# The first layer's first product as seven products on quadrants, in two PSUM banks per group

## The chip, the cores and the metric

The kernel runs on one core of one Trainium2 chip. The metric is the device time of one execution in microseconds (us). Of the core's engines, PE multiplies matrices, ACT and DVE work on vectors in the on-chip memory SBUF and in the accumulators of PSUM, POOL does a few reductions over partitions here, and SP issues the transfers. Each engine runs its own list of instructions in order; semaphores hold an instruction until others are done.

## The reference

Attention within chunks of 64 positions, then two feed-forward layers over 4608 tokens of width 512, each with 2048 hidden features:

```python
scores = scale * np.matmul(q_c, k_c.transpose(0, 1, 2, 4, 3))   # chunks of 64, 8 heads of 64
attn = np.exp(scores - np.max(scores, axis=-1, keepdims=True))
attn = attn / (np.sum(attn, axis=-1, keepdims=True) + 1e-09)
x = np.matmul(attn, v_c)                                        # as 4608 x 512
# first layer
h = x @ w_in
r = np.maximum(h, 0.0)
x = (s * (r * r) + b) @ w_out
# second layer
h = x @ w2_in
P = a[0] + a[1] * h + a[2] * h**2 + a[3] * h**3
Q = 1.0 + np.abs(b2[0]) * np.abs(h) + np.abs(b2[1]) * h**2
out = (P / (Q + 1e-06)) @ w2_out
```

## The kernel before

The tokens go in blocks: two of 256, computed in fp32 while the weights are still being made ready, then eight of 512 (j from 2 to 9). A hidden layer has 16 chunks f of 128 features. From block 2 on a product in near-fp32 precision is three fp16 matmuls (`TERMS`): an operand is split into a high half (a scaled copy, on ACT) and a low half (the rest, on DVE), and high x high, high x low and low x high are added in PSUM.

For a chunk f, `h_mm` (called by `l1_h`) runs 4 x 3 matmuls of 512 columns into one of two PSUM banks of the pool `ps_h`. ACT takes Relu of the bank into `r` (L429), squares it (L430) and writes its high half into `g` (L439); DVE subtracts for the low half (L440). The second product `l1_y` runs 12 matmuls of 512 columns that add chunk f into four PSUM banks `y`. In the program order the second product of a chunk comes one or two chunks after its first, so the other bank's product stands between.

The order is set by a list of slots, one for each chunk of each block (`seq1`). `at(slot, fn, ...)` files a job under a slot and `run_jobs` issues it there. So the softmax of the tiles of a later block, its scale c (`x_norm`, whose maximum over partitions is on POOL), its split into four pairs of halves (`x_split`, L379 and L380), the output of a finished block (`l1_out`, L474), its own scale and pieces for the second layer (`y_norm`, `y_split`) and the weights of the second layer are put between the chunks. These last are loaded raw from DRAM (`w2_load`, one load for two units of 128 x 512), decoded on DVE from 64-bit words to fp32 (L136 to L139: `bits`, `wf`) and written back ("parked"), during blocks 3 to 7. An amount `P0`, `PV0`, `WS`, `WP` sets how many slots before a block, or after which slot, such a job stands. ACT's chain for a tile of attention is L222, L236, L266 (exponential), L279 and L305 (x out of PSUM); DVE's is L264, L265, L273 to L280 and L306.

The second layer already has its first product by seven products on quadrants (Strassen's scheme in Winograd's form): a weight matrix and the input are both cut in 2 x 2 quadrants, seven sums or differences of the quadrants of each (`WORD` for the weights, `YORD` for the input) are split into halves, and seven products of half the size in each direction are added in three PSUM banks (`bZ`, `bY`, `bC`), with ACT copies between the banks. `PROD` names the two operands of each product. A unit of four chunks is a group there; its product form is L849.

What the two blocks of 256 tokens need first is the decoding of the first layer's weights in the order `units`, each through one of three buffers `bufs`; after them come the splits of these weights (`split`).

## Time and profile before

| | us |
|---|---|
| median of three runs | 1591.37 |
| lowest and highest run | 1589.68, 1595.19 |
| the profiled execution | 1593.01 |
| its span, first to last instruction | 1591.2 |
| PE busy | 1565.9 (98%) |
| DVE busy | 1232.2 (77%) |
| ACT busy | 921.8 (58%) |
| POOL busy | 25.7 (2%) |

The profile is of one execution; its rows give each instruction's or group's time, the idle time of its engine ahead of it, and what ended that idle time. The time from the first to the last instruction is 1.8 us under the time that was taken for this execution. The blocks of 512 tokens of the first layer run on PE from 149.5 to 870.6, the second layer from there to the end. A matmul's row overlaps the one behind it, so a run of twelve is measured from its start to the next one's start.

### The profile page before, as it was taken

To read this page: it belongs to the slowest core of one execution; us is meant where nothing else is said; L and a number is where in the kernel's file an instruction comes from. 1 tells how busy PE (TensorE), PEld (TensorE's weight loads), DVE (VectorE), ACT (ScalarE), POOL (GpSimd) and SP (SyncE) were. 2 spreads that over 40 slices of the span, in tenths; PEclk is the share of its full clock that TensorE was granted. 3 is DMA by queue.
4 is the path that set the end of the run, shared out by engine and by line. 5 is a ranking of instruction groups with operands and counts; after the bars stand their busy time and mean duration, and the time that the engine had idled before them with its cause. 6 is when DMAs were issued, how large, how long until landed. Compare 5 with 4: busy or idle time off the path is not lost.

```text
span 1591.2 us, 27221 instructions
## 1 busy us (share of the span) xinstructions
PE 1565.9 (98%) x11349; PEld 923.6 (58%) x11349; DVE 1232.2 (77%) x1886; ACT 921.8 (58%) x1296; POOL 25.7 (2%) x57
## 2 busy tenths in 40 slices
PE   8999999999999999999999899999999999999998
PEld 6887454444444444444445666666666666666664
DVE  7987448686777777364583999999998889888887
ACT  3676557374555646464675755555656565656564
POOL 0000000000000000000000000000000000000000
PEclk8999999999999999999999999999999999999999
DMA  7832216536354453111132010101010101010000
GB/s 283 280 87 76 52 42 199 172 108 178 107 165 136 136 149 98 42 34 54 54 114 86 34 60 27 47 27 47 27 47 27 48 27 47 27 47 34 20 27 27
DMA packets 86108, 131.27 MB, mean 83 GB/s; under 512 B 39648, under 2 KB 39648, under 8 KB 85984
## 3 DMA queue, kind: packets, MB, share of 16 engines
q1 hardware_dynamic: 85984, 129.53, 26.8%
q8 instruction: 89, 1.46, 0.4%
q14 instruction: 35, 0.29, 0.1%
HBM read 86.77 MB, written 34.34 MB: 76 GB/s over the span
## 4 chain that ended last, share of the span: by engine, by line
PE 73%; DVE 16%; issue 4%; DMA 4%; ACT 3%; POOL 0%; SPq 0%; POOLq 0%; ACTq 0%; DVEq 0%
PE y L907 19%; PE hp L414 16%; PE y L456 16%; PE bZ L849 9%; PE bY L849 5%; DMA raw<-in_moe_w_in_dram 2%; PE bC L849 2%; PE hp L424 1%; PE y L451 1%; DVE bits L138 1%; PE xp L301 1%; DVE wf L139 1%; DVE v L889 1%; DVE yhl L524 1%; PE sp L253 1%
## 5 line engine op out<-in xcount | busy, mean ns | idle before, releaser
L907 PE MATMUL y<-whl,g 128*128 128x512 f16 x1728 | 396.0, 379 | 3.0 <-DVE g L896 2.0
L414 PE MATMUL hp<-xhl,whl 128*128 128x512 f16 x1536 | 354.4, 380 | 2.5 <-ACT r L429 2.5
L456 PE MATMUL y<-g,whl 128*128 128x512 f16 x1536 | 352.5, 379 | 0.2
L849 PEld LDWEIGHTS <-whl 128*128 128x128 f16 x3024 | 296.6, 98 | 71.7 <-issue 7.8
L907 PEld LDWEIGHTS <-g 128*128 128x128 f16 x1728 | 168.7, 98 | 178.7 <-DVE g L896 4.4
L456 PEld LDWEIGHTS <-whl 128*128 128x128 f16 x1536 | 150.3, 98 | 181.8 <-issue 0.9
L414 PEld LDWEIGHTS <-whl 128*128 128x128 f16 x1536 | 146.1, 98 | 174.5 <-issue 4.5
L849 PE MATMUL bZ<-xhl,whl 128*128 128x256 f16 x1728 | 213.2, 273 | 2.1 <-ACT sn L855 1.1
L440 DVE TENSOR_TENSOR g<-r,g 128x512 f16<-128x512 f32 x128 | 88.0, 687 | 114.0 <-ACT g L439 113.9
L990 ACT ACTIVATE h<-bZ 128x512 f32<-128x512 f32 x36 | 21.4, 595 | 235.5 <-PE bZ L849 184.7
L429 ACT ACTIVATE r<-hp 128x512 f32<-128x512 f32 (+1 forms) x160 | 87.3, 546 | 106.3 <-PE hp L414 91.7
L873 DVE SCALAR_TENSOR_TENSOR v<-v,c 128x2048 f32<-128x2048 f32 (+1 forms) x42 | 85.8, 2044 | 37.3 <-ACT v L864 37.3
L849 PE MATMUL bY<-xhl,whl 128*128 128x256 f16 x864 | 106.2, 273 | 0.3 <-ACT sn L855 0.3
L430 ACT ACTIVATE r<-r 128x512 f32<-128x512 f32 (+1 forms) x160 | 93.5, 584 | 4.1
L874 DVE TENSOR_TENSOR e<-e,h 128x2048 f32<-128x2048 f32 (+1 forms) x42 | 83.1, 1981 | 11.3 <-ACT e L865 11.2
L888 DVE SCALAR_TENSOR_TENSOR g<-e,na,r 128x2048 f16<-128x2048 f32 (+1 forms) x42 | 85.7, 2045 | 6.0 <-ACT r L880 2.4
L875 DVE SCALAR_TENSOR_TENSOR e<-e,na,h 128x2048 f32<-128x2048 f32 (+1 forms) x42 | 85.7, 2045 | 0.8
L895 DVE SCALAR_TENSOR_TENSOR e<-e,na,v 128x2048 f32<-128x2048 f32 (+1 forms) x42 | 85.6, 2043 | 0.8
L889 DVE SCALAR_TENSOR_TENSOR v<-v,g 128x2048 f32<-128x2048 f32 (+1 forms) x42 | 83.2, 1984 | 1.0
L896 DVE TENSOR_TENSOR g<-e,r 128x2048 f16<-128x2048 f32 (+1 forms) x42 | 82.9, 1977 | 0.1
L439 ACT ACTIVATE g<-r 128x512 f16<-128x512 f32 x128 | 80.3, 628 | 3.1
L865 ACT ACTIVATE e<-h,na 128x2048 f32<-128x2048 f32 (+1 forms) x42 | 77.3, 1842 | 6.3 <-DVE g L896 6.3
(167 smaller groups left out, 1698.9 us busy)
## 6 DMA issues: line engine op xcount, KB each, us to landing
qk<-in_qk_dram SPq DMA_DIRECT2D x36, 512.0 KB, 3.8
raw<-in_moe_w_in_dram SPq DMA_DIRECT2D x16, 1024.0 KB, 5.5
raw<-in_moe_w_out_dram SPq DMA_DIRECT2D x16, 1024.0 KB, 5.4
v<-in_v_dram SPq DMA_DIRECT2D x36, 256.0 KB, 2.7
out_dram<-o SPq DMA_DIRECT2D x36, 256.0 KB, 2.1
yd<-yhl SPq DMA_DIRECT2D x27, 256.0 KB, 2.1
xhl<-yd SPq DMA_DIRECT2D x27, 256.0 KB, 2.7
w2din<-wf SPq DMA_DIRECT2D x16, 256.0 KB, 2.9
```

The source lines that it names most:

```text
L414: T.matmul(out=hp, lhsT=u[:, o:o + 128], rhs=x[kk][:, l, :], start=(m == 0), stop=(m == 3 * KD - 1))
L429: A.activation(out=r, in_=hp, func=AF.Relu, scale=1.0 if j < NFULL else C1)
L430: A.activation(out=r, in_=r, func=AF.Square)
L440: V.tensor_tensor(out=g[:, 1, :], in0=r, in1=g[:, 0, :], op=ALU.subtract)
L456: T.matmul(out=ybank[j][dd], lhsT=wo1.hl[f][:, o:o + 128], rhs=g[:, l, :], start=(f == 0 and m == 0), stop=(f == KF - 1 and m == 2))
L849: T.matmul(out=b[:, s, :], lhsT=w[:, a, o:o + 128], rhs=yin[j][pk][:, l, kk, :], start=start and s + kk + n == 0, stop=stop and s + kk + n ...
L873: V.scalar_tensor_tensor(out=v, in0=v, scalar=dlt, in1=v, op0=ALU.add, op1=ALU.mult)
L875: V.scalar_tensor_tensor(out=e, in0=e, scalar=na[:, 1:2], in1=hh, op0=ALU.add, op1=ALU.mult)
L888: V.scalar_tensor_tensor(out=g[:, 0], in0=e, scalar=na[:, 0:1], in1=r, op0=ALU.add, op1=ALU.mult)
L889: V.scalar_tensor_tensor(out=v, in0=v, scalar=q0c, in1=g[:, 0], op0=ALU.add, op1=ALU.mult)
L895: V.scalar_tensor_tensor(out=e, in0=e, scalar=na[:, 0:1], in1=v, op0=ALU.add, op1=ALU.subtract)
L907: T.matmul(out=ybank[j][t], lhsT=g[:, a, q, t * 128:(t + 1) * 128], rhs=w[:, l * 512:(l + 1) * 512], start=(u + q == 0 and m == 0), stop=( ...
```

## The change

From block 2 on, `l1_group` takes the place of `l1_h`. Its unit is four chunks, 2u, 2u+1, 2u+8 and 2u+9, which is two chunks from each half of the features. The seven products run as in the second layer, but with two banks, Z and Y, of the same pool `ps_h`:

1. Product 1 into Z, product 7 into Y. ACT copies Y to SBUF (`sn`, L504) and then Z into Y (L505).
2. Product 2 adds to Y, product 6 to Z. ACT takes Relu of Y (a quarter of the group's hidden values) and copies Z into Y again (L513).
3. Product 4 adds to Y, product 5 to Z. DVE adds `sn` to each of them into the half `h1` (L518, L519). ACT takes Relu, Square and the high half of 1024 columns, DVE the low half.
4. Product 3 adds to Z; Relu of Z, then Square and halves of the other 1024 columns.

Between the steps, `m2` runs the second product of a chunk of the group before, and `jobs_at` the slot's jobs. The input of a block is cut into seven pieces over four slots (`x_piece`) instead of four, and y pieces also go one by one. The first layer's weights are combined (28 combinations, `w1_combo`, through one helper `combo` for both layers) where they were split in 16 units. Decoding and loading go by quadrant (`FO`, `GO`), four raw loads are in flight at the start instead of three, attention's tiles stand at other distances from their block (`P0`, `PV0`), and several pools have fewer buffers: loads of attention 2 instead of 3, `bits` 1 instead of 2, the fetch of the last block's quadrants `wq` 1 instead of 2.

```diff
-    hl_p = ctx.enter_context(tc.tile_pool(name="hl", bufs=10, reuse_waits="tile"))
+    hl_p = ctx.enter_context(tc.tile_pool(name="hl", bufs=9, reuse_waits="tile"))
     wo1_p = ctx.enter_context(tc.tile_pool(name="wo1", bufs=KF + 1, reuse_waits="tile"))
+    wi1a_p = ctx.enter_context(tc.tile_pool(name="wi1a", bufs=14, reuse_waits="tile"))
...
-    wi1_p = left.enter_context(tc.tile_pool(name="wi1", bufs=KF + 1, reuse_waits="tile"))
+    wi1_p = left.enter_context(tc.tile_pool(name="wi1", bufs=14, reuse_waits="tile"))
     raw_p = left.enter_context(tc.tile_pool(name="raw", bufs=1, reuse_waits="tile"))
     l1_p = left.enter_context(tc.tile_pool(name="l1", bufs=2, reuse_waits="tile"))
-    ld_p = right.enter_context(tc.tile_pool(name="ld", bufs=3, side="right", reuse_waits="tile"))
+    ld_p = right.enter_context(tc.tile_pool(name="ld", bufs=2, side="right", reuse_waits="tile"))
...
+    FO = [0, 1, 2, 3, 8, 9, 10, 11, 4, 5, 6, 7, 12, 13, 14, 15]
+    GO = [f for u in range(4) for f in (2 * u + 8, 2 * u + 9, 2 * u, 2 * u + 1)]
...
-            self.order = [(kk, g) for g in range(KD) for kk in range(KD)] if kind == "in" else list(range(KF))
+            self.order = [(kk, g) for g in (0, 2, 1, 3) for kk in range(KD)] if kind == "in" else FO
...
-            t = raw_p.tile([128, 512], I32, name="bits", tag="bits", bufs=2)
+            t = raw_p.tile([128, 512], I32, name="bits", tag="bits")
...
+    def x_piece(j, p):
+        xhl.setdefault(j, {})[p] = piece(("x", j), xt[j][0], p, scx[j], hl_p, "xhl", 9)
+        if p == YORD[-1]:
+            xt.pop(j)
...
+    def product(w, x, u, p, b, start, stop=False):
+        wk, pk = PROD[p]
+        for s in range(2):
+            f = 2 * u + s
+            for kk in range(2):
+                t = w.sh[wk, kk, f // 4]
+                for n, (a, l) in enumerate(TERMS):
+                    o = (f % 4) * 128
+                    T.matmul(out=b[:, s, :], lhsT=t[:, a, o:o + 128], rhs=x[pk][:, l, kk, :],
+                             start=start and s + kk + n == 0, stop=stop and s + kk + n == 4,
+                             skip_group_check=True)
...
+    def l1_y2(j, u, q):
+        if u + q == 2 and u == 0:
+            ybank[j] = new_y()
+        first, last = (u, q) == (0, 2), (u, q) == (3, 1)
+        f = 2 * u + (q % 2) + 8 * (q // 2)
...
+    def l1_half(h, g):
+        hf = h.rearrange("p s b t -> p (s b t)")
+        A.activation(out=hf, in_=hf, func=AF.Square)
+        A.activation(out=g[:, 0], in_=hf, func=AF.Copy)
+        V.tensor_tensor(out=g[:, 1], in0=hf, in1=g[:, 0], op=ALU.subtract)
+
+    def l1_group(j, u, jobs_at, m2):
+        x = xhl[j]
+        bank = lambda nm: ps_h.tile([128, 2, 256], F32, name=nm, tag="h")
+        half = lambda: l1_p.tile([128, 2, 2, 256], F32, name="h1", tag="h1")
+        jobs_at(0)
+        Z, Y = bank("bZ"), bank("bY")
+        product(wi1, x, u, "1", Z, True)
+        product(wi1, x, u, "7", Y, True)
+        p7 = l1_p.tile([128, 2, 256], F32, name="sn", tag="sn", bufs=3)
+        A.activation(out=p7, in_=Y, func=AF.Copy)
+        A.activation(out=Y, in_=Z, func=AF.Copy)
+        m2(0)
+        jobs_at(1)
+        product(wi1, x, u, "2", Y, False)
+        product(wi1, x, u, "6", Z, False)
+        h0, h1 = half(), half()
+        g = gq[j, u] = l1_p.tile([128, 2, 2, 1024], F16, name="g", tag="g")
+        A.activation(out=h0[:, :, 0], in_=Y, func=AF.Relu, scale=16.0 * C1)
+        A.activation(out=Y, in_=Z, func=AF.Copy)
+        m2(1)
+        jobs_at(2)
+        product(wi1, x, u, "4", Y, False, True)
+        product(wi1, x, u, "5", Z, False)
+        V.tensor_tensor(out=h1[:, :, 0], in0=Y, in1=p7, op=ALU.add)
+        V.tensor_tensor(out=h1[:, :, 1], in0=Z, in1=p7, op=ALU.add)
+        h1f = h1.rearrange("p s b t -> p (s b t)")
+        A.activation(out=h1f, in_=h1f, func=AF.Relu, scale=16.0 * C1)
+        l1_half(h1, g[:, :, 1])
+        m2(2)
+        jobs_at(3)
+        product(wi1, x, u, "3", Z, False, True)
+        A.activation(out=h0[:, :, 1], in_=Z, func=AF.Relu, scale=16.0 * C1)
+        l1_half(h0, g[:, :, 0])
+        m2(3)
...
-        t = raw_p.tile([128, 4, 512], F32, name="wq", tag=("raw", "land")[len(quad) % 2])
+        t = raw_p.tile([128, 4, 512], F32, name="wq", tag="raw")
...
+    def w1_combo(q, p):
+        kk, g = q
+        t = [wi1.f32[u] for u in ((kk, g), (kk + 2, g), (kk, g + 2), (kk + 2, g + 2))]
+        combo(wi1, t, q, p, (w1sc, w1nsc), wi1.pool[g], ws_raw)
...
-    PV0 = 2
+    PV0 = 5
     WS, WP = 24, 4
-    P0, P1 = 2, (9, 6, 3, 0)
-    seq1 = [(0, f) for f in range(STAG)]
-    for f in range(KF):
-        seq1.append((1, f))
-        if f + STAG < KF:
-            seq1.append((0, f + STAG))
-    seq1 += [(j, f) for j in range(NFULL, NB) for f in range(KF)]
+    P0, P1 = 4, (9, 6, 3, 0)
...
-        at(slot + 1, x_split, j)
+        for m, p in enumerate(YORD):
+            at(slot + 1 + m // 2, x_piece, j, p)
...
-    bufs = ((y1_p, "y32"), (raw_p, "land"), (raw_p, "raw"))
+    bufs = ((y1_p, "y32"), (raw_p, "raw"), (l1_p, "g"), (l1_p, "g"))
...
+    for g, s0, n in ((0, 21, 10), (1, 32, 7)):
+        items = [((kk, g), p) for kk in range(2) for p in WORD]
+        for m, (q, p) in enumerate(items):
+            at(s0 + m * n // len(items), w1_combo, q, p)
+    for k, f in enumerate(GO):
+        at(max(pos[1, f] + 6, 30 + k), wo1.split, FO.index(f))
...
+        w1_load(6)
...
+        def y_later(j):
+            j2 = l1_out(j)
+            slot = start[j + 1] + (4 if j >= NFULL else 13)
+            at(slot + 1, y_norm, j2)
+            for m, p in enumerate(YORD):
+                at(slot + 2 + (m if j >= NFULL else m // 2), y_piece, j2, p)
...
+            for u in range(4):
+                l1_group(j, u, lambda n: l1_slot(start[j] + 4 * u + n), m2_of(prev))
+                prev = (j, u)
```

Two places in the order of instructions bear on what follows. The first is ACT around the x pieces of a block. Before, with `hp` the bank of a chunk's product, `c` the scale and `xhl` a piece:

```order
L305 ACTIVATE x_4204<-xp,xsc 128x4x128 [waits PE_49]
L236 ACTIVATE vs<-v,sc 128x512
L429 ACTIVATE r<-hp 128x512 [waits DVE_49,PE_49]
L379 ACTIVATE xhl<-x_4204,c_236 128x512 [waits DVE_49,Activation_49]
L430 ACTIVATE r<-r 128x512 [waits Activation_49]
L379 ACTIVATE xhl<-x_4204,c_236 128x512
L439 ACTIVATE g<-r 128x512 [waits Activation_49]
L379 ACTIVATE xhl<-x_4204,c_236 128x512 x2
L222 ACTIVATE wsq,am<-v 128x512 [waits DMAHW3_49,Pool_49]
L429 ACTIVATE r<-hp 128x512 [waits PE_49]
```

After, with `bZ` and `bY` the two banks, `sn` the copy of product 7 and `tx` a difference of quadrants:

```order
L492 ACTIVATE g<-h_5219 128x1024 [waits Activation_49]
L232 ACTIVATE wsq,am<-v 128x512 [waits DMAHW5_49,Pool_49]
L414 ACTIVATE xhl<-x_4395,c_239 128x512 [waits DVE_49]
L414 ACTIVATE xhl<-tx,c_239 128x512
L414 ACTIVATE xhl<-x_4395,c_239 128x512 [waits PE_49]
L504 ACTIVATE sn<-bY 128x512 [waits PE_49]
L414 ACTIVATE xhl<-x_4395,c_239 128x512
L505 ACTIVATE bY<-bZ 128x512 [waits Activation_49]
L512 ACTIVATE h_5534<-bY 128x2x256 [waits PE_49,Activation_49]
L414 ACTIVATE xhl<-x_4395,c_239 128x512
L276 ACTIVATE e<-e 128x512 [waits DVE_49]
L513 ACTIVATE bY<-bZ 128x512 [waits PE_49,Activation_49]
```

The pieces stood between the Square and the high half of one chunk; now three stand ahead of the copy of product 7 and one between it and the copy into Y, and the exponential (L276) stands ahead of the second copy into Y (L513).

The second is DVE at a decoding step of the second layer's weights, in the stretch with the scores' maxima (`mx`) of a tile. Before:

```order
L101 TENSOR_SCALAR apm<-amx 128x1 [waits Pool_49]
L103 TENSOR_SCALAR ape<-apm 128x1 [waits DVE_49]
L136 TENSOR_SCALAR bits<-raw 128x512 [waits DMAHW1_49]
L136 TENSOR_SCALAR bits<-raw 128x512
L440 TENSOR_TENSOR g<-r,g 128x512 [waits Activation_49]
L138 SCALAR_TENSOR_TENSOR bits<-raw,bits 128x512 [waits DVE_49] x2
L139 SCALAR_TENSOR_TENSOR wf<-raw,bits 128x512 [waits DMAHW2_49,DVE_49]
L264 TENSOR_REDUCE mx<-sp 128x4 [waits PE_49] x2
L265 TENSOR_TENSOR e<-sp,mx 128x4x64 [waits DVE_49] x2
```

After:

```order
L144 SCALAR_TENSOR_TENSOR wf<-raw,bits 128x512 [waits DMAHW5_49,DVE_49]
L493 TENSOR_TENSOR g<-h_4923,g 128x1024 [waits Activation_49]
L586 TENSOR_REDUCE am_223<-wf 128x1 [waits DVE_49]
L103 TENSOR_SCALAR apm<-amx 128x1 [waits Pool_49]
L105 TENSOR_SCALAR ape<-apm 128x1 [waits DVE_49]
L107 TENSOR_SCALAR inv<-ape 128x1 [waits DVE_49]
L108 RECIPROCAL sc<-inv 128x1 [waits DVE_49]
L141 TENSOR_SCALAR bits<-raw 128x512 [waits DMAHW7_49]
L143 SCALAR_TENSOR_TENSOR bits<-raw,bits 128x512 [waits DVE_49]
L144 SCALAR_TENSOR_TENSOR wf<-raw,bits 128x512 [waits DMAHW0_49,DVE_49]
L274 TENSOR_REDUCE mx<-sp 128x4 [waits PE_49] x2
L275 TENSOR_TENSOR e<-sp,mx 128x4x64 [waits DVE_49] x2
```

The scores' work followed the first bits step (which waits for a load, DMAHW) by a few rows, with a subtraction for `g` and the rest of the decoding between; now the whole decoding of a unit stands between the wait and the maxima, with no subtraction among it, and one buffer `bits` where there were two.

## Rows read from the trace of the kernel before

**Rows 1.** Busy time by stretch; columns: us from:to, busy us of each engine, granted clock.
```profile
43.00:160.00 117.00, 115.60 (x900) 95.08 (x899) 96.88 (x238) 81.71 (x178) 4.71 (x12) 1.00 0.48 141
...
300.00:655.00 355.00, 352.30 (x2740) 166.39 (x2739) 249.79 (x579) 199.36 (x345) 11.75 (x25) 1.00 0.45 132
...
1000.00:1591.00 591.00, 586.17 (x3912) 382.39 (x3910) 525.54 (x346) 335.38 (x308) 0.00 (x0) 1.00 0.12 36
```

**Rows 2.** The chain that ended last, by engine.
```profile
PE 73%; DVE 16%; issue 4%; DMA 4%; ACT 3%; POOL 0%; SPq 0%; POOLq 0%; ACTq 0%; DVEq 0%
```

**Rows 3.** Costliest groups: line, engine, operation, count, busy, mean ns, idle before.
```profile
L414 PE MATMUL hp<-xhl,whl 128*128 128x512 f16 x1536 | 354.4, 380 | 2.5 <-ACT r L429 2.5
```

**Rows 4.** PE around 510; start, length, engine, line, operation, count.
```profile
508.72 2.75 PE L414 MATMUL hp<-xhl,whl 128*128 128x512 f16 x12
511.31 2.75 PE L456 MATMUL y<-g,whl 128*128 128x512 f16 x12
```

**Rows 5.** PE in the second layer.
```profile
1062.73 1.47 PE L849 MATMUL bC<-xhl,whl 128*128 128x256 f16 x12
1064.05 1.47 PE L849 MATMUL bZ<-xhl,whl 128*128 128x256 f16 x12
```

**Rows 6.** What PE waited for from 160 to 1000.
```profile
PE bC L849 <- ACT bC L968: 2.9, 1, 2.9
PE hp L414 <- ACT r L429: 2.5, 2, 2.3
```

**Rows 7.** Groups of 300 to 655, each shape apart.
```profile
L440 DVE TENSOR_TENSOR g<-r,g 128x512 f16<-128x512 f32 x64 | 43.9, 686 | 18.6 <-ACT g L439 18.5
L439 ACT ACTIVATE g<-r 128x512 f16<-128x512 f32 x63 | 39.6, 628 | 1.6
...
L380 DVE SCALAR_TENSOR_TENSOR xhl<-x,c,xhl 128x512 f16<-128x512 f32 x16 | 11.6, 748 | 3.5 <-ACT xhl L379 3.5
...
L379 ACT ACTIVATE xhl<-x,c 128x512 f16<-128x512 f32 x16 | 11.0, 710 | 7.2 <-DVE c L106 7.2
...
L266 ACT ACTIVATE e<-e 128x512 f32<-128x512 f32 x16 | 10.1, 630 | 55.3 <-DVE e L265 55.3
...
L136 DVE TENSOR_SCALAR bits<-raw 128x512 int32<-128x512 int32 x26 | 9.9, 424 | 37.4 <-DMA raw<-in_moe_w_out_dram 20.5 <-DMA raw<-in_moe_w_in_dram 16.9
```

**Rows 8.** Groups of 1000 to 1591, each shape apart.
```profile
L982 DVE TENSOR_TENSOR h<-bZ,sn 128x512 f32<-128x512 f32 x29 | 19.8, 683 | 0.0
...
L855 ACT ACTIVATE sn<-bZ 128x512 f32<-128x512 f32 x29 | 17.3, 595 | 14.3 <-PE bZ L849 14.3
```

**Rows 9.** ACT from 505, in order of time.
```profile
505.83 0.67 ACT L305 ACTIVATE x<-xp,xsc 128x512 f32<-128x512 f32 x1
...
507.02 0.58 ACT L429 ACTIVATE r<-hp 128x512 f32<-128x512 f32 x1
509.77 0.72 ACT L379 ACTIVATE xhl<-x,c 128x512 f16<-128x512 f32 x1 [2.17 <-DVE c L106]
510.40 0.61 ACT L430 ACTIVATE r<-r 128x512 f32<-128x512 f32 x1
```

**Rows 10.** DVE in the same stretch.
```profile
509.51 0.17 DVE L106 RECIPROCAL c<-c 128x1 f32<-128x1 f32 x1
```

**Rows 11.** DVE from 310.
```profile
315.40 0.77 DVE L136 TENSOR_SCALAR bits<-raw 128x512 int32<-128x512 int32 x2 [2.90 <-DMA raw<-in_moe_w_in_dram]
```

**Rows 12.** ACT from 319.
```profile
319.93 0.63 ACT L266 ACTIVATE e<-e 128x512 f32<-128x512 f32 x1 [6.45 <-DVE e L265]
```

**Rows 13.** PE where the blocks of 512 tokens begin.
```profile
149.52 2.76 PE L414 MATMUL hp<-xhl,whl 128*128 128x512 f16 x12
```

**Rows 14.** DVE in the same stretch.
```profile
157.40 0.69 DVE L440 TENSOR_TENSOR g<-r,g 128x512 f16<-128x512 f32 x1
```

**Rows 15.** Busy time by stretch where the second layer begins.
```profile
880.00:890.00 10.00, 7.09 (x59) 5.93 (x58) 10.00 (x27) 8.48 (x15) 0.00 (x0) 0.93 0.22 80
890.00:900.00 10.00, 10.00 (x74) 7.56 (x73) 10.00 (x16) 7.20 (x13) 0.00 (x0) 0.90 0.00 0
```

More of the change, by code (lines that the diff above doesn't have):

```diff
@@ L194, in attn_moe_moe2 @@
     wo2 = Weight(w2_out, "out", wo1_p, "w")
+    wo2.order = list(range(KF))
     wi2.sh = {}
@@ L375, in norm_bound @@
         pow2_root(tot, inv, sc, nm + "p")
-    def split_hl(hl, x32, sc):
-        for a in range(KD):
-            A.activation(out=hl[a][:, 0, :], in_=x32[:, a, :], func=AF.Identity, scale=sc)
-            V.scalar_tensor_tensor(out=hl[a][:, 1, :], in0=x32[:, a, :], scalar=sc, in1=hl[a][:, 0, :],
-                                   op0=ALU.mult, op1=ALU.subtract)
     def x_norm(j):
@@ L403, in l1_consts @@
         V.tensor_tensor(out=alpha0, in0=wo1.inv, in1=s_sb, op=ALU.mult)
-    TERMS = ((0, 0), (0, 1), (1, 0))
-    def h_mm(w, x, f, n, tag, pool):
-        hp = pool.tile([128, n], F32, name="hp", tag=tag)
-        m = 0
-        for kk in range(KD):
-            u = w.hl[(kk, f // 4)]
-            for a, l in TERMS:
-                o = a * 512 + (f % 4) * 128
-                T.matmul(out=hp, lhsT=u[:, o:o + 128], rhs=x[kk][:, l, :], start=(m == 0), stop=(m == 3 * KD - 1))
-                m += 1
-        return hp
+        V.tensor_scalar(out=w1sc, in0=wi1.sc, scalar1=0.25, scalar2=None, op0=ALU.mult)
@@ L418, in l1_h @@
     def l1_h(j, f):
         n = blocks[j][1] * 128
-        if j < NFULL:
-            hp = ps_h.tile([128, n], F32, name="hp", tag="h")
-            o = (f % 4) * 128
-            for kk in range(KD):
-                last_mm[j, f] = T.matmul(out=hp, lhsT=wi1.f32[(kk, f // 4)][:, o:o + 128], rhs=xt[j][0][:, kk, :],
-                                         start=(kk == 0), stop=(kk == KD - 1))
-        else:
-            hp = h_mm(wi1, xhl[j], f, n, "h", ps_h)
-        r = l1_p.tile([128, n], F32, name="r", tag="r")
@@ L429, in l1_h @@
-        A.activation(out=r, in_=hp, func=AF.Relu, scale=1.0 if j < NFULL else C1)
+        hp = ps_h.tile([128, n], F32, name="hp", tag="h")
+        o = (f % 4) * 128
+        for kk in range(KD):
+            last_mm[j, f] = T.matmul(out=hp, lhsT=wi1.f32[(kk, f // 4)][:, o:o + 128], rhs=xt[j][0][:, kk, :],
+                                     start=(kk == 0), stop=(kk == KD - 1))
+        r = y1_p.tile([128, n], F32, name="r", tag="yhl", bufs=3)
+        A.activation(out=r, in_=hp, func=AF.Relu)
@@ L454, in l1_y, with new_y @@
+    def new_y():
+        return [ps_y.tile([128, 512], F32, name=f"y{dd}", tag=f"y{dd}") for dd in range(KD)]
+    gq = {}
+    def l1_y2(j, u, q):
[3 more added lines that the diff above has]
+        f = 2 * u + (q % 2) + 8 * (q // 2)
+        g = gq[j, u][:, :, q // 2, (q % 2) * 512:(q % 2 + 1) * 512]
+        for dd in range(KD):
             for m, (a, l) in enumerate(TERMS):
                 o = a * 512 + dd * 128
-                T.matmul(out=ybank[j][dd], lhsT=wo1.hl[f][:, o:o + 128], rhs=g[:, l, :],
-                         start=(f == 0 and m == 0), stop=(f == KF - 1 and m == 2))
+                T.matmul(out=ybank[j][dd], lhsT=wo1.hl[f][:, o:o + 128], rhs=g[:, l],
+                         start=(first and m == 0), stop=(last and m == 2))
+        if q == 1:
+            gq.pop((j, u))
@@ L782, in attn_moe_moe2, with m2_of, m2, l1_slot @@
             y_step()
-        for i in range(KF - 4, KF):
-            wo2.split(i)
+        prev = None
+        QO = (2, 3, 0, 1)
+        def m2_of(u):
+            def m2(n):
+                if u is None:
+                    return
+                l1_y2(*u, QO[n])
+                if u[1] == 3 and n == 3:
+                    y_later(u[0])
+            return m2
+        quads = [(kk, g) for g in range(2) for kk in range(2)]
+        wo2.todo, wo2.cut = list(GO), list(GO)
+        def l1_slot(slot):
+            j, k = slot // KF, slot % KF
+            run_jobs(slot)
+            if j == NB - 1:
+                if k >= 6:
+                    wo2.fetch(wo2.todo.pop(0))
+                if k >= 8:
+                    wo2.split(wo2.cut.pop(0))
+                for n in range(28 * k // KF, 28 * (k + 1) // KF):
+                    q = quads[n // 7]
+                    w2_combo(q, WORD[n % 7])
+                    if n % 7 == 6 and n // 7 + 1 < 4:
+                        w2_fetch(quads[n // 7 + 1])
+        for j in range(NFULL, NB):
+            if j == NB - 1:
+                right.close()
+                w2_p = ctx.enter_context(tc.tile_pool(name="w2", bufs=14, side="right", reuse_waits="tile"))
+                w2_fetch(quads[0])
+            for u in range(4):
+                l1_group(j, u, lambda n: l1_slot(start[j] + 4 * u + n), m2_of(prev))
+                prev = (j, u)
+        m2 = m2_of(prev)
+        for n in range(4):
+            m2(n)
+        while wo2.todo:
+            wo2.fetch(wo2.todo.pop(0))
+        while wo2.cut:
+            wo2.split(wo2.cut.pop(0))
         late = sorted(jobs)
@@ L838, in new_bank, with l2_product @@
             return bank[i, k]
[L840 to L851 removed]
+        def l2_product(i, p, b, start, stop=False):
+            product(wi2, yin[seq[i][0]], seq[i][1], p, b, start, stop)
         def snap(i, k, src):
```

207 lines of the change are left out of this document (85 added, 122 removed).

## The prediction

> **What bounds the kernel now.** I read the busy time by stretch first, then the chain that ended last, then the costliest groups, and last the order in time on PE, ACT and DVE around one group of the first layer. The stretches show PE busy 352.3 of 355 us in the middle of the first layer, with DVE at 249.8 and ACT at 199.4, and PE busy 586.2 of 591 us in the second layer, there with DVE at 525.5 [rows 1]. The chain is PE for 73% and DVE for 16% [rows 2]. So a shorter PE program shortens the run as long as the other engines deliver on time; they have room in the mean, and the question is whether they have it at each step.
>
> **What is removed from PE.** The first product of the first layer is 1536 matmuls of 512 columns, 354.4 us of busy time that overlaps, and it waited 2.5 us in all [rows 3]. Twelve of them take 508.72 to 511.31, 2.59 us [rows 4]; there are 128 such dozens, 331.5 us. After the change each group of four of the 16 feature chunks is seven products, P1 to P7, of twelve matmuls of 256 columns. The second layer has the same form: 1062.73 to 1064.05, 1.32 us [rows 5], 1.31 over several. 32 groups x 7 x 1.31 = 293.4 us. PE saves 38.1 us, and the 2.5 us that the old form waited [rows 6] go with it: 40.6.
>
> A rule of the Trainium skill speaks against that. "TensorE: Matmul & The Clock Gate", section "Back-to-back issue gap", gives for a stream of weight load and matmul 131 ns at 512 columns and 81 at 128, which would leave far more than half for 256 columns. An estimate midway on that page, about 98 ns, makes the new product 8.2 us against 6.3, about 60 us more over 32 groups and a sum near 1695. The rows do not bear it out: 216 ns and 110 ns [rows 4, 5]. The sum goes by the rows.
>
> **What is added to ACT and DVE.** In 355 us, 64 chunks pass [rows 7], so four chunks take 22.2 us. Before, those four cost DVE four subtractions of 0.69, 2.7 us [rows 7]. After, two subtractions of twice the size (at most 1.37 each) and two additions of PSUM (0.68 each [rows 8]): at most 4.1, some 3.8. ACT gets three more copies out of PSUM (0.6 each [rows 8]) and has fewer, larger Relu, Square and Copy: 0.9 more per group. The x of a block is cut in seven pieces instead of four: three more of 0.75 and four subtractions of 0.69 on DVE, some 5 us per block, three more of 0.71 on ACT [rows 7]. DVE then has about 71.5 us per block of 84 (four groups of 7 x 1.31, 4 x 2.59 for the second products, and about 1.45 for one attention tile). By the mean all this is hidden. It isn't by place: the two PSUM banks are used several times within one group, and PE now waits for ACT or DVE five times in each; before, the product of the next chunk stood in another bank, and PE seldom waited.
>
> **The blocks' x pieces.** Before, ACT stood still 2.17 us for the scale c, and the step behind it waited too: the Square L430 of a Relu that had ended at 507.60 ran only at 510.40 [rows 9]. PE did not feel it. After, the ACT rows shown for this place put three pieces, which wait for c, ahead of the copies `sn<-bY` and `bY<-bZ`, and a fourth between these two. P2, the second product into Y, waits for the last. Count from the end of the addition into h1 from Z. The Relu, Square and Copy of the half stand ahead of x on ACT (3.6 us), and from the start of x at 505.83 to c, ready at 509.68, it is 3.85 [rows 9, 10]; c is ready at 7.5 at the earliest, and about 10 where the two larger subtractions, the scores' work and the v split are ahead on DVE. Four pieces and two copies later (3.7 us) P2 may start: 11.2 to 13.7. PE's cover is P3, a dozen second products, P1, P7 and another dozen, 3 x 1.31 + 2 x 2.59 = 9.1, with 0.6 for the scores 9.7, plus up to 2 where PE and not DVE was late. The stall is 0 to 4 us; I take 2, the middle, in the seven blocks that have it: +14 (0 to 28).
>
> **The y pieces.** One group of a block has four output copies, and the next copies wait for three y pieces that need a scale of their own. P4 waits for the second Y copy. Its cover is P2, P6 and a dozen, 5.2 us; ACT needs three pieces (0.71), a Relu (0.59), the exponential (0.63 [rows 7]) and the copy, 3.9, plus its wait for the scale, which for x was 2.17 [rows 9]. That leaves 0.9 to 2.2; I take 1.3 in seven blocks: +9.1 (0 to 21).
>
> **The loads of the second layer's weights.** 16 loads are decoded on DVE in four blocks, and DVE stands 37.4 us for them, 2.3 each [rows 7]; one of them shows 2.90 [rows 11]. Behind such a wait stood the scores' work, and ACT's exponential came 6.45 us late [rows 12]; over 16 tiles ACT stood 55.3 us for it [rows 7]. In the old kernel that cost PE nothing. After, the exponential is ahead of the second Y copy (both pieces shown for ACT and DVE). P2, P6 and a dozen cover 5.2; maxima, exponential and copy need 2.7, so 2.5 is free. A wait of 2.3 with a decode of 1.8 passes it by 1.6 and with a queue ahead of it by 2.3. Only one of four groups of such a block has the wait right ahead of the scores: 4 x 2.3 = +9.2 (0, or 37 if all 16 groups have it).
>
> **The start.** PE comes to the blocks of 512 tokens at 149.5 [rows 13] and would, after six products (7.9) and about 5 us of earlier work, need the first additions at 162.4. DVE comes to its own place there at 157.4 [rows 14]. By the order it then has, ahead of the two additions, six more splits, 14 sums of weight quadrants, the three pieces and four differences of x, the additions, and work of one more attention tile: 9 x 0.75 + 20 x 0.69 + 4.5 = 25 us. Between 43 and 160 it was idle 20 us [rows 1]. If all of that is used, it is there at 162.4; if none, at 182. I take two thirds of it: 169, a stall of +6.5 (0 to 20).
>
> **The last block.** The combinations for the second layer are fetched into one buffer instead of two, with ACT nearly full; three waits for a landing, each cut to about 1.7 by what is queued ahead: +5 (0 to 12). The changed order of weight units, steps of four tiles in attention and fewer buffers for loads cost nothing in the sum: the products that use them lie several us behind the loads, and PE waited for none of them [rows 6].
>
> **The sum.** The profiled execution took 1593.0 us (span 1591.2). 1593.0 - 40.6 + 14 + 9.1 + 9.2 + 6.5 + 5 = 1596.2. It was 1.6 over the median of the runs, so 1594.6: no change that this kernel's measurement can tell (about 0.3%, 4.8 us). The gain on PE is real and is given back at the waits.
>
> **Rivals.** *The waits are hidden.* In the second layer the same form of product runs with DVE at 89%, and PE loses 4.8 of 591 us [rows 1], with three banks though, and nothing from DMA in it. On eight blocks of 84 us that rate is 5.5; with 3 at the start it is 1593.0 - 40.6 + 8.5 - 1.6 = 1559. For it: every stall of mine is the small difference of large numbers. Against it: in the first layer the small steps (POOL, loads, scales) are in line with the copies.
>
> *The scale decides.* c comes so late that ACT holds P2 back by 4 us in all seven blocks, from c over 10 us after the addition on; the lateness is handed to the next group's y pieces. +14 over the forecast: 1609, slower. For it: ACT's idle of 2.17 before c with a shorter DVE queue. Against it: the pieces' differences need no scale and may run ahead of it.
>
> *The clock falls.* After the one stall of 2.9 us [rows 6] the granted clock was 0.93 and 0.90 in two stretches of 10 us [rows 15], worth 1.7 us at the lower level of 1.2 GHz against 2.4. Were that so at 14 places (x and y groups of seven blocks), +24: 1618. The skill's page on the clock gate, section "A second HAM failure mode: psum-queue depth-cycling", says that PE cycling through PSUM banks can idle often enough for its clock to swing between the levels; here the second layer does so at a clock of 1.00 [rows 1].
>
> *The product is no faster,* if weight loads bind at 256 columns. Rows 5 speak against it; then, without the 38.1, 1633.
>
> **How the numbers follow.** Forecast (1582 to 1606): 0.46. Waits hidden (1551 to 1582): 0.31. Scale decides: 0.14. Clock: 0.06. No faster product: 0.03. Of the forecast's 0.46 some 0.08 lies under 1586.6, 0.20 within 4.8 of 1591.4, 0.18 above. Faster: 0.31 + 0.08 = 0.39; same: 0.20; slower: 0.18 + 0.14 + 0.06 + 0.03 = 0.41. The range leaves a tenth at each end: 1558 to 1612; the forecast's own is 1582 to 1606.
>
> **What would show it.** Right: twelve first-product matmuls at 1.31 us; PE's busy time 38 us less; between 160 and 870 PE waits of 30 to 55 us, most of them for ACT's copies out of Z into Y, in the groups with x or y pieces and in one group of each block with loads; blocks with loads some 4 us longer than those without. Wrong: PE waits under 15 us (the first rival), waits for DVE's additions in every group (DVE would then be the bound, which the sum does not have), or a granted clock under 0.97 in the first layer.

## The result, and the profile after

| | median us | lowest, highest | span of the profiled run | granted clock |
|---|---|---|---|---|
| before | 1590.53 | 1588.94, 1595.19 | 1591.2 | 0.994 |
| after | 1608.11 | 1605.38, 1610.48 | 1606.0 | 0.988 |

The change makes the kernel slower by about 1%: ratio 1.0105, 95% interval 1.0078 to 1.0132. The prediction gave 1594.6, a range of 1558 to 1612 and its largest share, 0.41, to slower.

The saving on PE is there. The busy time by stretch, after (to set beside [rows 1]):

```profile
43.00:160.00 117.00, 113.49 (x902) 95.67 (x901) 107.31 (x255) 78.56 (x171) 4.61 (x11) 0.99 0.41 136
...
300.00:655.00 355.00, 327.80 (x3185) 216.28 (x3183) 271.52 (x595) 208.87 (x310) 9.10 (x24) 0.98 0.39 125
...
1000.00:1591.00 591.00, 590.97 (x3969) 388.17 (x3968) 535.05 (x348) 340.77 (x311) 0.00 (x0) 1.00 0.11 34
```

In the stretch from 300 to 655 PE was busy for all but 3 us before and now stands still for 27, and the granted clock is 0.98; DVE and ACT have room, 272 and 209 of 355 us. In the second layer nothing of the sort is to be seen. The chain that ended last has changed with it [rows 2]:

```profile
PE 54%; DVE 26%; ACT 10%; DMA 5%; issue 5%; POOL 0%; SPq 0%; POOLq 0%; ACTq 0%; DVEq 0%
```

PE held 73% of the chain before, and DVE 16. The product's groups, with PE's idle time behind the second bar, where [rows 3] had 354.4 us in one (both layers are in one line now, so 1728 and 864 of these matmuls are the second layer's; each dozen still steps by 1.31 us):

```profile
L445 PE MATMUL bZ<-xhl,whl 128*128 128x256 f16 x3264 | 406.2, 275 | 2.8 <-ACT sn L937 1.1
...
L445 PE MATMUL bY<-xhl,whl 128*128 128x256 f16 x2016 | 252.1, 276 | 37.3 <-ACT bY L505 20.2
```

The first-layer waits of PE, by what it waited for; columns: total us, number, longest (two lines under 1 us are left out). Before there was one line of 2.5 us [rows 6].

```profile
PE bY L445 <- ACT bY L505: 20.2, 15, 2.8
PE bY L445 <- ACT bY L513: 14.7, 11, 3.2
PE bY L445 <- ACT h L526: 2.0, 2, 1.2
```

L505 and L513 are ACT's two copies of Z into Y. 34.9 of the 38.3 us that PE waited in the first layer are for these. P1 to P7 are the seven products of a group; P2 adds to the first of these copies and P4 to the second.

Where they come from is read in the order of time. First the group that leads into block 4, with the x pieces (an x group; each block has one). PE, then ACT:

```profile
319.87 0.69 PE L263 MATMUL sp<-qk 64*64 64x64 f32 x32
323.39 2.72 PE L445 MATMUL bY<-xhl,whl 128*128 128x256 f16 x12 [2.83 <-ACT bY L505]
325.90 1.85 PE L445 MATMUL bZ<-xhl,whl 128*128 128x256 f16 x12
```

```profile
318.64 0.63 ACT L232 ACTIVATE wsq<-v 128x512 bf16<-128x512 f32 x1 [1.50 <-DMA v<-in_v_dram]
...
319.81 0.72 ACT L414 ACTIVATE xhl<-x,c 128x512 f16<-128x512 f32 x1 [0.45 <-DVE c L391]
320.44 0.71 ACT L414 ACTIVATE xhl<-tx,c 128x512 f16<-128x512 f32 x1
321.06 0.71 ACT L414 ACTIVATE xhl<-x,c 128x512 f16<-128x512 f32 x1
321.67 0.57 ACT L504 ACTIVATE sn<-bY 128x512 f32<-128x512 f32 x1
322.14 0.71 ACT L414 ACTIVATE xhl<-x,c 128x512 f16<-128x512 f32 x1
322.76 0.58 ACT L505 ACTIVATE bY<-bZ 128x512 f32<-128x512 f32 x1
```

P2 at 323.39 waited 2.83 us for the copy that ended at 323.34. That copy stood behind four x pieces, the first of which waited for the scale c (0.45), and ahead of them the sum of squares of v had waited 1.50 for a transfer. The next row shows a second cost: the dozen matmuls of P2 took 323.39 to 325.90, 2.51 us instead of 1.31.

Then the group before it, in which weights of the second layer are decoded. DVE, ACT and PE:

```profile
300.06 0.43 DVE L141 TENSOR_SCALAR bits<-raw 128x512 int32<-128x512 int32 x1 [4.13 <-DMA raw<-in_moe_w_in_dram]
...
301.86 0.75 DVE L274 TENSOR_REDUCE mx<-sp 128x4 f32<-128x256 f32 x2
302.53 0.75 DVE L275 TENSOR_TENSOR e<-sp,mx 128x256 f32<-128x256 f32 x2
```

```profile
294.00 0.63 ACT L232 ACTIVATE wsq<-v 128x512 bf16<-128x512 f32 x1 [2.14 <-DMA v<-in_v_dram]
...
303.31 0.63 ACT L276 ACTIVATE e<-e 128x512 f32<-128x512 f32 x1 [5.28 <-DVE e L275]
303.84 0.58 ACT L513 ACTIVATE bY<-bZ 128x512 f32<-128x512 f32 x1
```

```profile
295.88 1.47 PE L445 MATMUL bY<-xhl,whl 128*128 128x256 f16 x12 [1.22 <-ACT bY L505]
...
298.49 2.75 PE L484 MATMUL y<-g,whl 128*128 128x512 f16 x12
304.48 1.47 PE L445 MATMUL bY<-xhl,whl 128*128 128x256 f16 x12 [3.23 <-ACT bY L513]
```

The wait of 1.22 us at 295.88 goes back to v again (2.14 at 294.00). Then DVE stood 4.13 us for the raw load, with the scores' maxima (L274) behind it; so the exponential came at 303.31, after 5.28 us of waiting, and the copy behind it at 303.84, and PE, which had run out at 301.25, waited 3.23 us. Before, a wait of DVE of this kind (2.90 us [rows 11]) stood ahead of an exponential that ACT got 6.45 us late [rows 12], at no cost to PE.

The loss can be laid out for blocks 3 to 6, in which all 32 units are decoded (259 to 613), from the start of one group's P7 to that of the same group four blocks on: 244.31 to 624.35, 380.0 us. A group without a stall takes 21.24 us, so 16 take 339.8, and 40.2 were lost (before, the four blocks took some 357):

| in blocks 3 to 6 | waits of PE, us |
|---|---|
| first copy in the x groups, behind the x pieces and the jobs for v (2.83, 2.82, 1.15, 2.82) | 9.6 |
| second copy behind a raw load (3.23, 1.82, 2.24, 2.07, 1.56) | 10.9 |
| first copy behind the sum of squares of v, in the group before the x group (1.22, 0.90, 0.80, 1.17) | 4.1 |
| y outputs, y pieces and others | 6.0 |
| no wait recorded: matmuls at the lower clock, small gaps | 9.5 |

On the whole, the second layer begins at 870.6 before and 884.2 after, 13.5 later in spite of 40.6 saved: 54.1 us lost, 13.9 of them outside blocks 3 to 6. Block 7, the first without decoding, took 86.0 us, against 95.0 for one of blocks 3 to 6 in the mean.

### The profile page after: what moved, and what is told of

Same layout as the page of the kernel before. It is cut to its first block, busy times and chain, and to the rows that moved or that the text cites. A ratio compares the mean times of both kernels' runs of the same rounds, so it can differ in the third digit from the quotient of the medians.

```text
span 1606.0 us, 29660 instructions
## 1 busy us (share of the span) xinstructions
PE 1540.4 (96%) x12501; PEld 1042.7 (65%) x12501; DVE 1315.2 (82%) x1980; ACT 966.9 (60%) x1268; POOL 21.9 (1%) x57
## 4 chain that ended last, share of the span: by engine, by line
PE 54%; DVE 26%; ACT 10%; DMA 5%; issue 5%; POOL 0%; SPq 0%; POOLq 0%; ACTq 0%; DVEq 0%
PE y L989 21%; PE bZ L445 13%; PE bY L445 8%; PE y L484 6%; PE bC L445 2%; DVE bits L143 2%; DVE wf L144 2%; ACT h L491 2%; DVE yhl L415 2%; DMA raw<-in_moe_w_in_dram 1%; ACT g L492 1%; DMA raw<-in_moe_w_out_dram 1%; ACT h L521 1%; DVE bits L141 1%; DVE whl L620 1%
## 5 line engine op out<-in xcount | busy, mean ns | idle before, releaser
L445 PEld LDWEIGHTS <-whl 128*128 128x128 f16 x5712 | 560.2, 99 | 164.7 <-issue 50.8
L445 PE MATMUL bZ<-xhl,whl 128*128 128x256 f16 x3264 | 406.2, 275 | 2.8 <-ACT sn L937 1.1
L445 PE MATMUL bY<-xhl,whl 128*128 128x256 f16 x2016 | 252.1, 276 | 37.3 <-ACT bY L505 20.2
L484 PEld LDWEIGHTS <-whl 128*128 128x128 f16 x1536 | 150.3, 98 | 156.6 <-issue 2.1
L1071 ACT ACTIVATE h<-bZ 128x512 f32<-128x512 f32 x36 | 21.4, 595 | 235.6 <-PE bZ L445 188.4
L493 DVE TENSOR_TENSOR g<-h,g 128x1024 f16<-128x1024 f32 x64 | 78.3, 1223 | 75.9 <-ACT g L492 75.8
L946 ACT ACTIVATE v<-h,bc 128x2048 f32<-128x2048 f32 (+1 forms) x42 | 73.6, 1756 | 7.7 <-DVE h L1065 6.5
L961 ACT ACTIVATE r<-v,c 128x2048 f32<-128x2048 f32 (+1 forms) x42 | 73.5, 1755 | 1.0 <-DVE v L955 1.0
L962 ACT ACTIVATE r<-r,c 128x2048 f32<-128x2048 f32 (+1 forms) x42 | 73.3, 1755 | 1.0
L491 ACT ACTIVATE h<-h 128x1024 f32<-128x1024 f32 x64 | 67.5, 1054 | 1.6
L492 ACT ACTIVATE g<-h 128x1024 f16<-128x1024 f32 x64 | 67.5, 1054 | 1.6
```

Of the source, the lines that this page charges most:

```text
L445: T.matmul(out=b[:, s, :], lhsT=t[:, a, o:o + 128], rhs=x[pk][:, l, kk, :], start=start and s + kk + n == 0, stop=stop and s + kk + n == 4 ...
L484: T.matmul(out=ybank[j][dd], lhsT=wo1.hl[f][:, o:o + 128], rhs=g[:, l], start=(first and m == 0), stop=(last and m == 2))
L491: A.activation(out=hf, in_=hf, func=AF.Square)
L492: A.activation(out=g[:, 0], in_=hf, func=AF.Copy)
```

## The experiments

Each is the changed kernel with the edit shown; times are medians, ratios are to the kernel before, with 95% intervals. The first question was whether the stalls come from the order in which small waits stand on ACT and DVE, or from DVE having too much to do.

**1. The decoding behind the scores.** `WS` sets the slot of the loads and of their decoding, so both come two slots later as well.

```diff
-    WS, WP = 24, 4
+    WS, WP = 26, 4
...
+            with tc.issue_after(last(nc.vector.engine)):
+                w.decode(i, raw_p, "wf")
```

> The changed kernel with each decoding step of the second layer's weights (DVE) issued behind the scores' differences instead of ahead of them, and the load jobs two slots later; nothing left out. Theory (in-order waits): the copy Z into Y stands on ACT behind the exponential, which stands behind DVE's wait for a raw load. Its stalls in the changed kernel (3.23, 1.82, 2.07, 1.56 and 2.24 us, 10.9 in all, and some 3.5 us at the lower clock behind them) go: 1608 - 14 = 1594, between 1590 and 1600. PE's waits for the second copy L513 fall from 14.7 to about 4 us. Rival (DVE has too much to do in blocks 3 to 6, whatever its order): the decoding now delays the additions, and the time stays at 1604 to 1610.

Measured: 1588.02 us, ratio 0.9965 (0.9954 to 0.9977). PE's waits, the same lines:

```profile
PE bY L445 <- ACT bY L505: 21.0, 19, 2.5
PE bY L445 <- ACT bY L513: 3.6, 7, 0.8
```

The second copy's waits fall from 14.7 to 3.6, as the theory had it, and the first copy's stay (20.2, now 21.0). The time fell by 20, 6 more than expected and 2 past the end of its range; the clock from 300 to 655 was 1.00 instead of 0.98, which by an estimate is worth some 7 us of that stretch (0.02 of 355). DVE's work is the same, so the rival falls.

**2. One raw load, all decoding on that tile.**

```diff
+        if n == 0:
+            with tc.issue_after(last(nc.sync.engine)):
+                w.load(i, raw_p, "raw")
+            one_raw.extend(w.raw[w.order[m]] for m in range(2))
+        for m in range(2):
+            w.raw[w.order[i + m]] = one_raw[m]
```

> The changed kernel with one raw load of the second layer's weights instead of 16; every decoding step works on that one tile, so the second layer's weights are not the reference's. DVE's work is unchanged, only its wait for the transfer goes. Theory (in-order waits): as in the run with the decoding behind the scores, some 14 us less, 1594 (1589 to 1599), no wait of DVE for raw data, and PE's waits for L513 at about 4 us. Rival (DVE's amount of work): 1603 to 1609. Rival (the stalls are the scale c's and the v loads' alone): 1605 to 1609.

Measured: 1596.25 us, ratio 1.0018 (1.0008 to 1.0029).

```profile
PE bY L445 <- ACT bY L505: 16.1, 18, 2.4
PE bY L445 <- ACT bY L513: 7.4, 10, 1.4
PE bZ L445 <- DVE h L519: 3.6, 5, 1.4
```

12 us less, in the theory's range, with all of DVE's work kept: the loads alone, by DVE's wait for them or by their traffic, which this run takes away together, account for that. But 7.4 and not 4 us are still waited for the second copy, and now 3.6 for additions, so the decoding itself seems to stand in the way too.

**3. No decoding.** As in 2, and all but the first unit's decoding and maxima left out (DVE 227.8 us busy in the stretch from 300 to 655 instead of 271.5).

> The changed kernel with one raw load and one decoding step of the second layer's weights; the others are left out with their maxima, so DVE has 2.5 us per unit of 128 x 512 less for 31 units, 77 us, and no wait for raw data; the writing back stays. Theory (in-order waits): what is left are the x and y pieces and v: 1585 to 1594, little under the 1596 with one load and all decoding. Rival (DVE's amount of work in blocks 3 to 6 is the bound): far under it, 1565 to 1580.

Measured: 1583.82 us, ratio 0.9941 (0.9921 to 0.996). It is 1 us under the theory's range and 4 over the rival's; the 12 us that 77 us of DVE's work are worth are more than I had said. So with the jobs in this order the amount of DVE's work counts for something as well, besides where it stands. But PE still waits 15.0 us for the first copy with DVE at 64%, in the profiled execution, which at 1588.2 us was the longest of seven: the x pieces and v.

**4. The copies ahead of the jobs, on ACT.**

```diff
-        A.activation(out=Y, in_=Z, func=AF.Copy)
+        c1 = A.activation(out=Y, in_=Z, func=AF.Copy)
         m2(0)
-        jobs_at(1)
+        with tc.issue_after(c1.ins):
+            jobs_at(1)
```

and the same for the second copy and `jobs_at(2)`.

> The changed kernel with an order on ACT alone: the jobs between the product steps (x and y pieces, exponential) are issued behind the copy Z into Y that PE waits for. Theory (in-order waits): the x groups' stalls (11.2 us and some 5 at the lower clock) and those behind the exponential (10.9 and 3.5) go, and the pieces and the probabilities come later, which costs up to 6: 1578 to 1588. What is left is the wait for v. Rival (DVE's amount of work, or its lateness): PE then waits for DVE's additions instead, 1600 to 1610.

Measured: 1583.01 us, ratio 0.9939 (0.9919 to 0.9959).

```profile
PE bZ L445 <- DVE h L521: 7.8, 8, 2.1
PE bY L445 <- ACT bY L505: 7.3, 12, 1.2
...
PE bY L445 <- ACT bY L514: 0.7, 1, 0.7
```

25 us less with no work taken away: in the range. The waits for the two copies fall from 34.9 to 8.0 (L514 is the second copy here); in the x groups of blocks 3 to 6 PE waits for neither, though the sum of squares of v still stands ahead of the first. 7.8 us are now at DVE's additions, most of them in the x groups. That the pieces make these late is not shown: with the decoding moved as well (run 7) they are 3.0.

**5. v later.** `((-8, at_amax), (-7, at_split)` became `((-6, at_amax), (-5, at_split)`.

> The changed kernel with the sum of squares of v (ACT L232, which waits for the v load) and the split of v two slots later. Theory: in four groups with a load of second-layer weights SP issues v late, and the wait of ACT for it (1.75 to 2.14 us) stalls PE at the first copy by 0.8 to 1.2 us, 4.1 in all; with the lower clock up to 6 with those that add to the x groups. 1602 to 1605. Rival (the copy waits for the scale c or for PE anyway): 1607 to 1610.

Measured: 1609.97 us, ratio 1.0103 (1.0084 to 1.0122). The sum of squares of v still stood ahead of both copies in ACT's order, since the scheduler moves it forward; ACT waited 32.6 us for v. So this run told nothing of v. It was repeated with the order forced:

```diff
+            if fn is at_amax and copy1:
+                with tc.issue_after(copy1[0]):
+                    fn(*args)
```

> The changed kernel with one edit: the sum of squares of v is now forced behind the copy Z into Y (the earlier run with v alone left ACT's order as it was), its split two slots later. Theory: ACT's waits for v (26.1 us in the changed kernel) no longer stand ahead of the copies; the stalls of 0.8 to 1.2 in the four groups with y pieces go, and the x groups' by up to 1: 1599 to 1604. Rival (the copy waits for the scale c, the v wait is hidden beside it): 1606 to 1610.

Measured: 1601.53 us, ratio 1.0055 (1.0039 to 1.007).

```profile
PE bY L445 <- ACT bY L514: 18.7, 14, 3.3
PE bZ L445 <- DVE h L520: 5.5, 5, 1.5
PE bY L445 <- ACT bY L506: 3.5, 3, 1.3
```

(L506 is the first copy here, L514 the second.) The first copy's waits fall from 20.2 to 3.5 and 4 us come back at the second copy, 5 at the additions: 6.6 us in all, in the theory's range. But the theory had 4.1 us of the first copy's waits and up to 1 for each x group, and 16.7 went. In the x groups of blocks 3 to 6 PE no longer waits for the first copy at all, though in this run three pieces still stand ahead of the copy of product 7 on ACT and a fourth ahead of the first copy. So in the changed kernel the stalls of the x groups there (9.6 us) needed both the pieces and the jobs for v: runs 4 and 5 each move one of them, and either is enough.

**6. A third buffer for v.** The trace of after shows SP issuing a v load 0.77 us after the start of a v split, each time, so I took the pool's cut from three buffers to two as the cause.

```diff
-        x = ld_p.tile([128, 2, NP, D], F32, name="v", tag="v")
+        x = ld_p.tile([128, 2, NP, D], F32, name="v", tag="v", bufs=3)
```

and one buffer of the copy of product 7 less.

> The changed kernel with three buffers for v again instead of two (room from one of three buffers of the copy of product 7); no order is forced, but the scheduler now puts both copies into Y of the x groups ahead of the x pieces. Theory (the cut of buffers made v late: in the changed kernel SP issues v 0.77 us after the start of the split that frees its buffer, five times of five): ACT's wait for v ahead of the copies (26.1 us) falls under 8, the four groups with y pieces lose their 4.1 us of stall, and the x groups, by the new order, most of 11.2 and the lower clock behind them: 1590 (1586 to 1600). Rival (v is late because it stands in SP's queue behind the raw loads and their writing back): ACT waits for v as before, 1600 to 1608.

Measured: 1609.11 us, ratio 1.011 (1.0093 to 1.0127). SP's issues of v, the splits on DVE and the sums of squares on ACT in that run:

```profile
293.21 0.33 SPq L221 DMA_DIRECT2D v<-in_v_dram  x1
...
319.00 0.33 SPq L221 DMA_DIRECT2D v<-in_v_dram  x1
```

```profile
292.44 0.74 DVE L247 SCALAR_TENSOR_TENSOR vs<-v,sc,vs 128x512 f16<-128x512 f32 x1
...
318.24 0.74 DVE L247 SCALAR_TENSOR_TENSOR vs<-v,sc,vs 128x512 f16<-128x512 f32 x1
```

```profile
296.11 0.63 ACT L232 ACTIVATE wsq<-v 128x512 bf16<-128x512 f32 x1 [2.03 <-DMA v<-in_v_dram]
...
321.77 0.63 ACT L232 ACTIVATE wsq<-v 128x512 bf16<-128x512 f32 x1 [3.60 <-DMA v<-in_v_dram]
```

The load is still issued 0.77 us after the start of a split, and ACT waits 34.0 us for v. The theory of the buffer falls. The trace of before could have told it: there, with three buffers, every v load from 160 to 870 is issued 0.76 to 0.80 us after the start of a split, and ACT waits 52.2 us for v, where it waits 26.1 in the changed kernel.

```profile
307.58 0.74 DVE L237 SCALAR_TENSOR_TENSOR vs<-v,sc,vs 128x512 f16<-128x512 f32 x1
308.35 0.33 SPq L211 DMA_DIRECT2D v<-in_v_dram  x1
```

What the load waits for is open; the rival (SP's queue) isn't shown either. The run shows one thing more. ACT's order came out another one here: in the x groups the first copy stands ahead of all pieces, with only v's sum of squares ahead of it. Even so, PE waits there at both copies, in the one at 321.77 for 2.04 and 2.00 us, the first behind the wait of 3.60 for v, the second behind pieces and the exponential:

```profile
PE bY L445 <- ACT bY L505: 19.5, 19, 2.6
PE bY L445 <- ACT bY L513: 17.2, 9, 3.0
```

**7. Combinations.** The copies first, with v forced behind the first copy; the copies first with the decoding behind the scores; all three; all three with a third v buffer.

> The copies into Y ahead of the jobs on ACT, and with them the sum of squares of v behind the first copy, which the run with v alone did not achieve (ACT's order stayed). Theory: PE's 7.3 us at the first copy (L505), which stand behind the wait for v, go: 1576 (1572 to 1579). Rival (the split of v, now later, holds up the additions or the probabilities instead): 1581 to 1586.

> The copies into Y ahead of the jobs on ACT and the decoding behind the scores' differences on DVE. Theory: with the copies first, no copy stands behind the exponential any more, so the decoding's place gains little, at most the 2 to 3 us by which the additions in the x groups are late: 1581 (1577 to 1586). Rival (the two effects add up): 1563 to 1570.

> The changed kernel with three edits of order: the copies into Y ahead of the jobs on ACT, the decoding behind the scores' differences on DVE, and the sum of squares of v behind the first copy; nothing left out. Theory (in-order waits): of what the run with the copies alone still waited for, 7.3 us at the first copy (behind the wait for v) and part of the 7.8 at DVE's additions go: 1583 - 9 = 1574 (1568 to 1580). Rival (DVE's amount of work now decides in blocks 3 to 6): PE's waits move to the additions, 1580 to 1588.

> The run with all three edits of order (1567.4) with three buffers for v as well. Theory: with the sum of squares of v behind the copies nothing of PE waits for v, so the third buffer gains nothing: 1567 (1565 to 1569). Rival (v's split still holds up attention, and with it PE at the first groups): 1560 to 1564.

| copies first and | us | ratio (interval) |
|---|---|---|
| v | 1573.89 | 0.9881 (0.9851 to 0.9911) |
| decoding | 1578.82 | 0.992 (0.9892 to 0.9948) |
| v and decoding | 1567.42 | 0.9841 (0.9814 to 0.9868) |
| v, decoding, third v buffer | 1565.16 | 0.9833 (0.9818 to 0.9847) |

The first two came as expected, the third 7 us better. The second and the third differ by v alone, 11 us: PE's waits for the first copy are 12.5 and 0.7 us in them. With all three, the stretch of blocks 3 to 6 is

```profile
300.00:655.00 355.00, 353.10 (x3518) 234.60 (x3516) 299.65 (x651) 228.50 (x339) 11.83 (x26) 1.00 0.51 143
```

with PE busy for 353.1 of 355 us, at a clock of 1.00, and DVE at 299.7, more than in the changed kernel. Its blocks 3 to 6 took 340.5 us, against 339.8 without any stall. The third buffer makes no difference that the intervals tell. So the loss in these blocks, all but 0.7 us, comes from where small jobs stand in the engines' order, and a version with all three beats both kernels.

**8. Less work ahead of the first group.** The run with all three edits, less 12 of the 16 sums and differences of the first layer's weight quadrants.

```diff
+            if w is not wi1:
                 V.tensor_tensor(out=src, in0=src, in1=a11, op=ALU.subtract)
```

> The run with all three edits of order (copies, decoding, v; 1567.4), with 12 of the 16 sums and differences of the first layer's weight quadrants left out, so the weights of four of seven products are wrong: DVE has 12 x 0.69 = 8.3 us less, nearly all of it ahead of the first additions. Theory (DVE comes late to the first group, which has no second products to cover it): PE's waits in the first two groups, 4.6 us in the run with all three edits, fall by half or more: 1563 to 1565.5. Rival (the start is set by ACT's splits and the fp32 blocks): 1566 to 1569.

Measured: 1565.34 us, ratio 0.9839 (0.9821 to 0.9857). What PE waited for from 150 to 200 in the run with all three edits:

```profile
PE y L484 <- ACT g L492: 1.5, 1, 1.5
PE bZ L445 <- DVE h L520: 1.1, 1, 1.1
PE bY L445 <- ACT bY L514: 1.0, 1, 1.0
PE bY L445 <- ACT bY L505: 0.7, 1, 0.7
PE sp L263 <- ACT x L315: 0.3, 1, 0.3
```

Of these 4.6 us, the waits for DVE's addition and for g go (2.6), and 2.4 are left. The ratio is that of the run with all sums (0.9841), so the time doesn't tell; that DVE's sums make half of these waits is shown by the waits alone.

## Why the prediction was right and where it fell short

The mechanism was right: PE's gain is real and is given back at the copies. The sum was too small: its single number, 1594.6, was 13.5 too low, and the measured 1608.1 lies 2 above the forecast's own range (1582 to 1606), inside the whole one (1558 to 1612). The direction was hardly forecast: 0.41 for slower stood beside 0.39 for faster, and the single number was for no change.

- *PE saves 38.1 us, 1.31 us a dozen.* Right: the steps are 1.31, and the run almost without stalls in blocks 3 to 6 is as long as these steps make it. PE's busy time, which was to be 38 us less, fell by 25.5 (1565.9 to 1540.4); behind some stalls matmuls were longer (last section), the rest is not laid out. The figures of the Trainium skill, "TensorE: Matmul & The Clock Gate", section "Back-to-back issue gap", for a stream of matmuls (131 ns at 512 columns, 81 at 128), by which the product would have become longer, don't hold here: it is 216 ns at 512 columns [rows 4] and 109 at 256.
- *The stalls are at the copies of Z into Y, in order, behind x and y pieces and behind loads.* Right: 34.9 of 38.3 us, and run 4, which changes ACT's order alone, takes all but 8.0 of them away.
- *Sizes.* For blocks 3 to 6 the sum had x pieces 8.0 (four of the seven), y pieces 5.2, loads 9.2. Measured 9.6, 6.0 (the y outputs with it) and 10.9. The rest of the layer had 21.4 in the sum and lost 13.9: the last block, put at 5, waited some 3, and x and y cost little in blocks 7 and 8, which have no loads. For the blocks without loads the sum had the path wrong: it took the x pieces to stall all seven blocks by 2 us each, but the x groups of blocks 2, 7 and 8 waited 0.8, 0.8 and 0 for the first copy. Blocks with loads were to be some 4 us longer than those without; they were 9.
- *The start.* It was put at 6.5, for DVE's first additions. PE came to these blocks at 158.9 and not at 149.5, and in the first group it waited 3.4 us, for ACT's two copies and a Relu (2.27, 0.24 and 0.85), and for no addition.
- *"fewer buffers for loads cost nothing in the sum".* This step failed in what it looked at. I took it from PE, which waited for no load. But ACT waited for v before as well, and a wait of ACT was now to stand ahead of the copies. The sum of squares of v in the old kernel, 300 to 655:

```profile
L222 ACT ACTIVATE wsq<-v 128x512 bf16<-128x512 f32 x16 | 9.9, 621 | 44.8 <-DMA v<-in_v_dram 44.8
```

Its 44.8 us cost PE nothing there. Now such a wait stands ahead of a copy: 4.1 us in blocks 3 to 6 by the trace, a part of the 9.6 in the x groups, and 6.6 us in all by the run with v forced. The cut of buffers is not shown to make v late, and run 6 and the trace of before speak against it.
- *The clock.* It was a rival with a price of 1.7 us a place and a chance of 0.06, and 0 in the sum. In blocks 3 to 6, 9.5 us went without a recorded wait; some 6 of that are longer matmuls behind four of the stalls (last section), and the clock of 0.98 from 300 to 655 gives some 7 by estimate. The rest is open. So a part of this rival came together with the forecast, and the sum had left it out. The Trainium skill ("TensorE: Matmul & The Clock Gate", section "A second HAM failure mode: psum-queue depth-cycling") has PE that cycles through PSUM banks stand idle between matmuls often enough for its clock to swing between the levels. The changed kernel, at 0.98, agrees with that; the run with all three edits cycles through the same two banks from 300 to 655 at 1.00, so the cycling alone, without the stalls, does not do it.
- *The scale decides* (1609, 0.14) came to the right number by luck, on another road: the x groups were at 2.8 at most and in four blocks, not at 4 us in seven, and the loads, v and the clock made up the rest.

In sum, blocks 3 to 6 have 13.6 that the sum had at nothing (4.1 and 9.5) and 4.1 that it had too small (1.6, 0.8, 1.7); the rest of the first layer has 7.5 less than the sum, the second layer 1.2 more, and the median lies 2.1 over the profiled span where the forecast had 0.2. That makes 13.3 of the 13.5. So the steps of the sum that failed are the two that it put at nothing, ACT's wait for v and the clock; the terms that it had were each within 2 us in these blocks.

## What to carry to other kernels

When a change makes PE wait for small copies several times in a group, list for each copy what stands ahead of it on its engine and what those instructions wait for (scales, transfers, another engine's wait), also where the old kernel shows such waits at no cost. Take the order of the built program, not the one written: the scheduler put the pieces ahead of copies that were written earlier, and an edit of slots alone did nothing for v, where the same with an explicit order took 7 us off, and the order of the copies alone 25. Before trading work for fewer waits, try the order.
